# A Fourier convolution's last tile: its scratch in three parts instead of four, and a different reload

## The chip, the cores and the metric

One core of one Trainium2 chip runs the whole program. The metric is the device time of one execution in microseconds; lower is better. The compute engines are TensorE (PE in the profile; its weight loads are listed apart as PEld), VectorE (DVE), ScalarE (ACT) and GpSimd (POOL). SyncE (SP) issues most DMA transfers, ScalarE's queue (ACTq) a few. Engines run in parallel and wait for each other through semaphores.

## The reference

The reference convolves an image with a 7 x 7 kernel through Fourier transforms, circularly, over 96 input and 96 output channels:

```python
H = W = 224; C = 96; K = 7
x: (1, H, W, C) bf16        w: (K, K, C, C) bf16

wp = jnp.pad(w, ((0, H - K), (0, W - K), (0, 0), (0, 0)))
Xf = rfft2(x as float32, axes=(1, 2))
Wf = rfft2(wp as float32, axes=(0, 1))
Yf = jnp.einsum('bhwi,hwio->bhwo', Xf, Wf)
y  = irfft2(Yf, s=(H, W), axes=(1, 2)).astype(bfloat16)
```

## The kernel before, in words

The kernel does not transform the whole image. It cuts the 224 rows into NJ = 8 blocks of B = 28 rows and transforms each block, with 6 rows of overlap, along the rows only, to NS = 17 pairs of values (an index s from 0 to 16, each with two parts r). Along the columns it convolves directly, with a fast scheme of short taps. The 224 columns are cut into NT = 7 tiles of 32 columns; a tile has TW = 16 column pairs (index w), each with an even and an odd column.

For each tile t three stages follow:

- Stage A (`a_jobs`, `f_jobs`) multiplies the rows of the image by the transform matrix Fm into the tile xf.
- Stage B (`b_round`, one call for each s) multiplies sums of xf (the J tiles, made by VectorE) by the transformed weights WF, in about forty products of 96 columns a round, and puts the result into yf: 128 partitions are (w, j), and a row of yf is s. Every three s (`YGRP`, `YGRPL`) a *put* writes yf to a scratch tensor in DRAM, laid out as w, j, s, (r, column parity, channel).
- Stage C reads the scratch back with j, s and r on the partitions (the *reload*; each row of one w is 384 bytes) and multiplies by the inverse matrix G, which gives pixels. They are evicted as bf16 and stored to `out`.

Stage C of a tile normally runs as small jobs among the rounds of the next tiles. Round by round the order is written out by hand: lists of jobs with due times (`add`, `pace`), and every engine's instructions keep program order (`_Ordered`).

The last tile, t = TL = 6, has no later rounds to hide in. Its scratch is a set of tensors, cut along s by `SLAST` (line 37), here (0, 9, 12, 15, 17). Part 0 (`scra`, s 0 to 8) is reloaded early, in round s = SA + 2 = 11 (lines 964 to 967), into two views `tl_a[0]` and `tl_a[1]` (line 720) of a free xf buffer, one for each half of the row blocks (g = 0: j 0 to 3, g = 1: j 4 to 7). Each half has KA = 72 rows (4 blocks x 9 s x 2), widened to KAP = 80 with eight rows of the other half, for which the matrix GA has zeros. Parts 1 to 3 (`scrb`) are reloaded after the rounds by `load_b` (lines 723 and 724), one DMA each, into `tl_b`, 128 rows in all: 48, 48 and 32. The puts of the last tile's first five groups (three s each) are issued from ScalarE's queue (`puts`, lines 659 and 696), the last one, of s 15 and 16, from SP.

After the rounds the program issues, in this order: the remaining jobs of stage C for tile 5 (lines 971 and 972), `load_b` for each part (974 and 975), four stores of tile 5's pixels held back till now (`outs`, 976), and the last tile's own stage C. That needs sixteen results (g, q) of 112 x 384. Each is the sum of two products: `first` (GA with part 0, contraction over part 0's rows) and `second` (GB with the 128 rows of the other parts). Eight `first` products run ahead, into the eight banks of PSUM. Then WARM = 26 *fillers*, products of zeros that add nothing to the last bank, keep PE at work until the reloads land. Then the `second` products follow, each with its eviction, interleaved with the eight `first` products that are left; every two results make one store, eight in all.

GA and GB are made from G by small copies through DMA (`g_parts`, lines 726 to 737), one for each round of tiles 3 and 4 (lines 962 and 963) until none is left.

Of the kernel before, what the change touches and what calls it, by code (L numbers as in the profile page):

```python
# [8 lines left out]
BF16 = mybir.dt.bfloat16  # L9
# [5 lines left out]
B = 28  # L15
# [18 lines left out]
PGRP = ((0, 5), (5, 8), (8, 11), (11, 14), (14, 17))  # L34
YGRP = ((0, 3), (3, 6), (6, 9), (9, 12), (12, 15), (15, 17))
YGRPL = ((0, 3), (3, 6), (6, 9), (9, 12), (12, 15), (15, 17))
SLAST = (0, 9, 12, 15, 17)
SA = SLAST[1]
YMAX = 3
YBUF = 4  # L40
# [5 lines left out]
SH3 = (0, 8, 17)  # L46
MERGE = ()
NP2 = 0
WARM = 26
HEAD = ("w",) * 6 + ("x0", "w", "w", "h0", "h1", "w", "w", "x1", "w", "w")  # L50
W1 = 30
ZC = 48
# [12 lines left out]
def kernel(  # L65
# [7 lines left out]
    _, H, W, C = x.shape  # L73
    assert tuple(w.shape) == (KT, KT, C, C) and C == 96 and H == NJ * B and W % (2 * TW) == 0
    NT = W // (2 * TW)
    TL = NT - 1
# [29 lines left out]
    VE, SE, GE, TE, DE = (_Ordered(e) for e in (nc.vector, nc.scalar, nc.gpsimd, nc.tensor, nc.sync))  # L106
# [9 lines left out]
    def bank():  # L116
        return pools["psb"].tile([128, 512], F32, name="pb")
# [30 lines left out]
    def dma(out_ap, in_ap):  # L148
        return DE.dma_start(out=out_ap, in_=in_ap)
# [7 lines left out]
    G = cpool.tile([3 * FR, 3 * B], BF16, name="Gm")  # L157
    KA = 4 * 2 * SA
    NL = len(SLAST) - 1
    KB = [NJ * 2 * (SLAST[i + 1] - SLAST[i]) for i in range(1, NL)]  # L160
    RB = [sum(KB[:i]) for i in range(NL - 1)]
# [33 lines left out]
    def load_x(t, jg):  # L195
        return load_rows(xbuf(t, jg), jg, t * 2 * TW, 2 * TW)
# [208 lines left out]
    def diff(s):  # L405
        def f():
            load["v"] += 60 + C * NTAP / 1.92
            w0, w1, w2 = (WF[0:C, slot(s, r)].rearrange("i t o -> i (t o)") for r in range(3))
            VE.tensor_tensor(out=w2, in0=w0, in1=w1, op=ALU.subtract)
        return f  # L410
# [113 lines left out]
    def then_load(f, t, jg):  # L524
        def g():
            f()
            if t < NT:
                load_x(t, jg)
        return g
# [65 lines left out]
    def b_round(t, s, mid, end, ydve=False, planes=()):  # L595
# [90 lines left out]
        if s == y1 - 1:  # L686
            dst, yo0 = scr_tiles[t], 0
            if t == TL:
                i = sum(s >= v for v in SLAST[1:])
                dst, yo0 = scr_tiles[(t, i)], SLAST[i]  # L690

# [8 lines left out]
    scr_tiles = {}  # L700
# [15 lines left out]

    TW2 = 2 * TW * C
    tl_all = xf_bufs[(TL + 1) % 2].rearrange("c p r s w j -> c (p r s w j)")
    KAP = -(-KA // 16) * 16
    tl_a = [tl_all[0:KAP, g * TW2:(g + 1) * TW2].rearrange("p (w e) -> p w e", e=2 * C) for g in range(2)]  # L720
    tl_b = tl_all[:, 2 * TW2:3 * TW2].rearrange("p (w e) -> p w e", e=2 * C)

    def load_b(i):
        dma(tl_b[RB[i]:RB[i] + KB[i]], scr_tiles[(TL, 1 + i)].rearrange("w j s (r e) -> (j s r) w e", r=2))

    def g_parts():
        for g in range(2):
            for j in range(4):
                p = g * (KAP - KA) + j * 2 * SA
                dma(GA[p:p + 2 * SA, g, j * B:(j + 1) * B], G[0:2 * SA, 0:B])  # L730
                yield
        for j in range(NJ):
            for i in range(NL - 1):
                s, s1 = SLAST[i + 1:i + 3]
                n = 2 * (s1 - s)
                dma(GB[RB[i] + j * n:RB[i] + (j + 1) * n, j // 4, j % 4 * B:(j % 4 + 1) * B], G[2 * s:2 * s1, 0:B])
                yield
# [105 lines left out]
    def fills(qs, k):  # L843
        def f():
            for q in qs:
                pace(q, k)
        return f
# [3 lines left out]
    def add(a, b, jobs):  # L851
        qs.append([a, b, jobs, len(jobs)])
# [15 lines left out]
    for r in range(NS + LAG):  # L868
        if r == 0:
            for i in range(1, PGRP[0][1]):  # L870
                add(max(2 * i - 3, 0), 2 * i - 1, [diff(i)])
            for i in range(N5, REAL[1]):
                add(2 * i - (3 if i % 3 == 0 else 2), 2 * i - (i % 3 == 0), [diff(i)])
            add(0, 4, fj[1][0] + fj[1][1])
            add(8, 12, fj[2][0] + fj[2][1])
        if r == 2:
            new_xf(1, SH2[0], SH2[1])
        for p in range(3):
            if r == (1, 3, 6)[p]:
                if p:  # L880
                    new_xf(1, SH2[p], SH2[p + 1])
                else:
                    xf_tiles[1] = xf_bufs[1]
                fj = f_jobs(1, p)
                if p == 2:
                    for jg in range(2):
                        fj[jg][-1] = then_load(fj[jg][-1], 2, jg)
                add((4, 7, 12)[p], (7, 11, 15)[p], fj[0] + fj[1])
        for p in range(2):
            if r == SH3[p + 1] + 1 - p:  # L890
                new_xf(2, SH3[p], SH3[p + 1])
                fj = f_jobs(2, p)
                if p:
                    for jg in range(2):
                        fj[jg][-1] = then_load(fj[jg][-1], 3, jg)
                add(2 * r, 2 * r + (12, 5)[p], fj[0] + fj[1])
        if r == PGRP[-2][1] + 1:
            assert not any(q[2] for q in qs[:len(PGRP) - 1])
            wtmp_cm.__exit__(None, None, None)
            t_pool = ctx.enter_context(tc.tile_pool(name="tt", bufs=NTT, side="right"))  # L900
            t2_pool = ctx.enter_context(tc.tile_pool(name="tt2", bufs=1, side="right"))
            yo_pool = ctx.enter_context(tc.tile_pool(name="yo", bufs=2, side="right"))
            g_pool = ctx.enter_context(tc.tile_pool(name="gp", bufs=1, side="right"))
            GA = g_pool.tile([KAP, 2, 4 * B], BF16, name="GA")
            GB = g_pool.tile([128, 2, 4 * B], BF16, name="GB")
            GE.memset(GA[:], 0.0)
            GE.memset(GB[:], 0.0)
        if r == 3:
            g_fin()
        for t in range(2):  # L910
            s = r - LAG * t
            if not 0 <= s < NS:
                continue
            now = bursts.pop((r, t), ())
            now = jit(*now) if now else []
            now, rest = rest + now[:2], now[2:]
            both = LAG <= r < NS
            b_round(t, s, fills(qs, 2 * r + (t if both else 0)), fills(qs, 2 * r + (t if both else 1)), False, now)
            if r == 0:
                for d in load_x(1, 1):  # L920
                    tc.add_manual_dep(d.ins, held_x.ins.name, SYNC, reason="second half behind the first products")
# [8 lines left out]
    for t in range(2, NT):  # L930
        if t == TL:
            scr_tiles[t] = None
            scr_tiles[(t, 0)] = dr_pool.tile([TW, NJ, SA, 4 * C], BF16, name="scra")
            for i in range(1, NL):
                scr_tiles[(t, i)] = dr_pool.tile([TW, NJ, SLAST[i + 1] - SLAST[i], 4 * C], BF16, name=f"scrb{i}")
        else:
            scr_tiles[t] = dr_pool.tile([TW, NJ, NS, 4 * C], BF16, name="scr")
        qs = []
        if t + 1 < NT:
            add(4 if t == 2 else 0, 26, a_jobs(t + 1))  # L940
        nold, nnew = CQ[t]
        k1 = 2 * NS if t < TL else 2 * NS - 8
        k0 = {2: 15, TL: 6}.get(t, 3)
        km = k0 + -(-(k1 - k0) * nold // (nold + nnew))
        add(k0, km, cj[:nold])
        cn = c_jobs(t - 1)
        cj = cn[nnew:]
        add(km, k1, cn[:nnew])
        plan = {}
        for g, (s0, s1) in enumerate(JGB):  # L950
            if g + 1 < len(JGB) or t + 1 < NT:
                plan[s0 if g + 1 < len(JGB) else s0 - 1] = g
        for s in range(NS):
            now = ()
            if s in plan:
                g = plan[s]
                now = jit(t, g + 1) if g + 1 < len(JGB) else jit(t + 1, 0)
            if s == 2 and t == 2:
                queue_c(0)
            if s == (3 if t in (2, TL) else 2):  # L960
                queue_c(t - 1)
            if t in (3, 4):
                next(gp, None)
            if t == TL and s == SA + 2:
                sv = scr_tiles[(TL, 0)].rearrange("w j s (r e) -> (j s r) w e", r=2)
                for g in range(2):
                    dma(tl_a[g], sv[g * (2 * KA - KAP):g * (2 * KA - KAP) + KAP])
            b_round(t, s, fills(qs, 2 * s), fills(qs, 2 * s + 1), bool(now) or (t == TL and s >= NS - 3), now)
    tail[0] = 1
    load["v"], load["a"] = 1000.0, 0.0  # L970
# [12 lines left out]

    def first(g, q):
        pc = bank()[0:M4, 0:4 * C]
        TE.matmul(pc, lhsT=GA[:, g], rhs=tl_a[g][:, 2 * q:2 * q + 2, :].rearrange("p w e -> p (w e)"), start=True, stop=False)
        return pc

    def second(g, q, pc, yo):
# [3 lines left out]
    live = {k: first(*k) for k in order[:8]}  # L993
    for _ in range(WARM):
        TE.matmul(live[order[7]].rearrange("p (a b) -> p a b", a=3), lhsT=wu[:, 0:M4], rhs=wu[:].unsqueeze(1).to_broadcast([128, 3, 128]),
                  start=False, stop=False)
# [44 lines left out]
```

## Time and profile before

| | us |
|---|---|
| median of the runs | 263.75 (263.49 to 264.52) |
| profiled execution | 263.47 |
| its span, first to last instruction | 261.7 |
| PE busy | 252.0 (96%) |
| DVE busy | 218.4 (83%) |
| ACT busy | 196.7 (75%) |
| POOL busy | 97.6 (37%) |
| DMA, mean rate over the span | 179 GB/s |

Times in the profile are microseconds from the span's start. A row of the timeline has the start, the length, the engine, the operation with its tiles, and in brackets the idle time before it and what ended that. In a row of the chain the work is the one that the next step waited for. A DMA's issue is listed on the queue that issues it (SPq, ACTq); its data follow later, on sixteen DMA engines that all queues share, as packets. All lines of the kernel appear as L99, since a helper there records every operation, so that groups are told apart by their tiles: pb is a bank of PSUM, wu the zeros of the fillers, scra and scrb the parts of the last tile's scratch, tt the stores' buffers.

### The profile page before, as it was taken

The numbers are of one execution on the slowest core, as the hardware profiler recorded it, in microseconds if no ns is written. First come the engines' busy times: TensorE is split into PE (matmuls) and PEld (weight loads), VectorE is DVE, ScalarE is ACT, GpSimd is POOL, SyncE is SP. The second block draws the span as 40 slices with busy tenths as digits, with TensorE's granted clock in tenths as the row PEclk, the third lists the DMA queues.
The fourth block names the chain that finished last, engine by engine and source line by source line (L and its number), as shares of the span: only waits on it lengthen the run. The fifth ranks groups of instructions, "written<-read, shape, count | busy, mean of one in ns | idle before, by whom it ended". The sixth has DMA issues, their size and how long they took to land.

```text
span 261.7 us, 11987 instructions
## 1 busy us (share of the span) xinstructions
PE 252.0 (96%) x5054; PEld 233.2 (89%) x5054; DVE 218.4 (83%) x462; ACT 196.7 (75%) x470; POOL 97.6 (37%) x152
## 2 busy tenths in 40 slices
PE   8999999999999999999999999999999999989983
PEld 2889999999989999989999998999999999979652
DVE  6799998899999889868887788878989799989724
ACT  8889978697745967988988799887988853555423
POOL 7782224464656633232223322334123423423000
PEclk9999999999999999999999999999999999999999
DMA  7995104611111697997967596878849842886996
GB/s 177 272 186 135 48 6 140 177 48 48 48 51 71 183 255 138 302 286 192 271 188 222 143 278 206 212 200 255 275 139 193 288 140 83 206 232 185 236 249 201
DMA packets 47278, 46.88 MB, mean 179 GB/s; under 512 B 35696, under 2 KB 38452, under 8 KB 47224
## 3 DMA queue, kind: packets, MB, share of 16 engines
q1 hardware_dynamic: 46504, 44.64, 62.6%
q10 hardware_dynamic: 720, 1.47, 1.7%
q8 instruction: 39, 0.64, 1.1%
q14 instruction: 15, 0.12, 0.2%
HBM read 24.76 MB, written 21.33 MB: 176 GB/s over the span
## 4 chain that ended last, share of the span: by engine, by line
PE 74%; DVE 10%; DMA 8%; issue 4%; ACT 1%; POOL 1%; SPq 1%; DVEq 0%; ACTq 0%
PE pb L99 68%; PE ps L99 6%; DVE J L99 5%; DMA xn<-in_x_dram 3%; DVE WF L99 2%; DMA tt<-scr 2%; DMA xf<-scrb 2%; DMA scrb<-yf 1%; DVE v L99 1%; POOL yf L99 1%; DVE yf L99 1%; DMA scr<-yf 1%; DVE u L99 1%; SPq L99 1%; ACT xf L99 0%
## 5 line engine op out<-in xcount | busy, mean ns | idle before, releaser
L99 PE MATMUL pb<-WF,J 96*128 96x96 bf16 x2821 | 162.4, 206 | 2.1 <-DVE u L99 0.8
L99 PEld LDWEIGHTS <-J 96*128 96x128 bf16 x2821 | 138.0, 98 | 11.0 <-issue 3.7
L99 POOL TENSOR_TENSOR yf<-v,u 128x384 bf16<-128x384 f32 x79 | 81.4, 1044 | 139.7 <-issue 86.3
L99 ACT CAST xf<-pb 96x408 bf16<-96x408 f32 (+6 forms) x140 | 65.1, 492 | 3.4 <-PE pb L99 1.4
L99 PE MATMUL pb<-WF,xf 96*128 96x96 bf16 x952 | 59.9, 206 | 0.2
L99 DVE TENSOR_TENSOR J<-xf 96x456 bf16<-96x456 bf16 (+3 forms) x85 | 56.0, 698 | 0.0
L99 PEld LDWEIGHTS <-xf 96*128 96x128 bf16 x952 | 47.1, 98 | 1.0 <-PE ps L99 0.6
L99 PE MATMUL pb<-Fm,xn 118*128 118x136 bf16 (+4 forms) x576 | 43.8, 203 | 0.2 <-DMA xn<-in_x_dram 0.2
L99 PE MATMUL pb<-tt,Gm 102*84 102x384 bf16 (+1 forms) x132 | 32.0, 326 | 0.5 <-DVE yf L99 0.4
L99 ACT CAST yo<-pb 84x384 bf16<-84x384 f32 (+1 forms) x61 | 26.2, 482 | 6.2 <-PE pb L99 6.2
L99 PEld LDWEIGHTS <-xn 118*128 118x128 bf16 x576 | 28.6, 97 | 0.5 <-issue 0.4
L99 ACT CAST J<-pb 84x384 bf16<-84x384 f32 (+1 forms) x64 | 27.5, 491 | 0.0
L99 DVE TENSOR_TENSOR J<-J 96x912 bf16<-96x912 bf16 (+2 forms) x42 | 25.4, 604 | 0.0
L99 ACT CAST WF<-pb 96x480 bf16<-96x480 f32 x42 | 21.3, 566 | 0.1
L99 PEld LDWEIGHTS <-wq 128*128 128x128 bf16 (+1 forms) x288 | 19.7, 148 | 0.2
L99 DVE TENSOR_TENSOR yf<-v,u 128x384 bf16<-128x384 f32 x26 | 15.2, 583 | 0.9
L99 PE MATMUL pb<-wq 128*128 128x120 bf16 x192 | 15.3, 224 | 0.0
L99 DVE TENSOR_TENSOR WF<-WF 96x960 bf16<-96x960 bf16 x15 | 14.0, 931 | 1.4 <-ACT WF L99 1.3
L99 PEld LDWEIGHTS <-Gm 102*84 102x84 bf16 (+1 forms) x132 | 11.3, 117 | 1.6 <-issue 0.6
L99 PEld LDWEIGHTS <-wu 128*112 128x112 bf16 (+1 forms) x49 | 6.2, 128 | 6.4 <-issue 3.9
L99 ACT COPY xf<-xf 96x816 bf16<-96x816 bf16 (+4 forms) x18 | 10.8, 659 | 0.0
L99 DVE CAST tt<-pb 112x384 bf16<-112x384 f32 x8 | 4.2, 555 | 6.6 <-PE pb L99 6.2
(397 smaller groups left out, 256.9 us busy)
## 6 DMA issues: line engine op xcount, KB each, us to landing
scr<-yf SPq DMA_DIRECT2D x30, 288.0 KB
xn<-in_x_dram SPq DMA_DIRECT2D x12, 672.0 KB
tt<-scr SPq DMA_DIRECT2D x24, 336.0 KB
out_dram<-yo SPq DMA_DIRECT2D x12, 252.0 KB
out_dram<-J SPq DMA_DIRECT2D x12, 252.0 KB
tt<-scr SPq DMA_DIRECT2D x6, 288.0 KB
wq<-in_w_dram SPq DMA_DIRECT2D x5, 288.0 KB
WF<-in_x_dram SPq DMA_DIRECT2D x2, 672.0 KB
```

The costliest lines, as they stand in the source:

```text
L99: r = fn(*a, **k)
```

## The change

The last tile's scratch is cut into three parts instead of four, so that s 9 to 14 are one tensor and one reload of 96 rows; its puts stay three s each. Part 0's reload brings both halves g side by side, 72 rows with 32 elements of 384 bytes each, in two DMAs that are cut at row 64; GA loses its padding and its second copy. `first` reads its columns of half g with a step. GA and GB need 4 + 16 small copies instead of 8 + 24. The fillers are 18 instead of 26.

```diff
-SLAST = (0, 9, 12, 15, 17)
+SLAST = (0, 9, 15, 17)
...
-WARM = 26
+WARM = 18
...
-    KAP = -(-KA // 16) * 16
-    tl_a = [tl_all[0:KAP, g * TW2:(g + 1) * TW2].rearrange("p (w e) -> p w e", e=2 * C) for g in range(2)]
+    tl_a = tl_all[0:KA, 0:2 * TW2].rearrange("p (w g e) -> p w g e", g=2, e=2 * C)
...
     def g_parts():
-        for g in range(2):
-            for j in range(4):
-                p = g * (KAP - KA) + j * 2 * SA
-                dma(GA[p:p + 2 * SA, g, j * B:(j + 1) * B], G[0:2 * SA, 0:B])
-                yield
+        for j in range(4):
+            dma(GA[j * 2 * SA:(j + 1) * 2 * SA, j * B:(j + 1) * B], G[0:2 * SA, 0:B])
+            yield
...
-            GA = g_pool.tile([KAP, 2, 4 * B], BF16, name="GA")
+            GA = g_pool.tile([KA, 4 * B], BF16, name="GA")
...
             if t == TL and s == SA + 2:
-                sv = scr_tiles[(TL, 0)].rearrange("w j s (r e) -> (j s r) w e", r=2)
-                for g in range(2):
-                    dma(tl_a[g], sv[g * (2 * KA - KAP):g * (2 * KA - KAP) + KAP])
+                sv = scr_tiles[(TL, 0)].rearrange("w (g j) s (r e) -> (j s r) (w g) e", g=2, r=2)
+                ta = tl_a.rearrange("p w g e -> p (w g) e")
+                for p0, p1 in ((0, KA // 16 * 16), (KA // 16 * 16, KA)):
+                    dma(ta[p0:p1], sv[p0:p1])
...
     def first(g, q):
         pc = bank()[0:M4, 0:4 * C]
-        TE.matmul(pc, lhsT=GA[:, g], rhs=tl_a[g][:, 2 * q:2 * q + 2, :].rearrange("p w e -> p (w e)"), start=True, stop=False)
+        TE.matmul(pc.rearrange("p (w e) -> p w e", w=2), lhsT=GA[:], rhs=tl_a[:, 2 * q:2 * q + 2, g], start=True, stop=False)
         return pc
```

## The prediction

> **What bounds the kernel now.** I read the page's shares first (PE is busy for 96% of the span), then PE's own waits, then the chain that ended last, in order of time, and last the queues and the DMA packets of the final 25 us.
>
> PE's waits from 150 us to the end are three:
>
> ```profile
> PE pb L99 <- DMA xf<-scrb: 1.2, 1, 1.2
> PE pb L99 <- DVE u L99: 0.8, 1, 0.8
> PE pb L99 <- DVE yf L99: 0.4, 1, 0.4
> ```
>
> Columns: total us, times, longest. So up to the tail PE is the bound, and what the change takes off SP's queue before the tail (small DMAs into GA and GB) frees nothing that PE waits for. PE's instructions are the same in both programs, in the same order, but for eight fillers. The whole change is therefore read from the tail. Its chain (start, us, what):
>
> ```profile
> 244.94 3.54 DMA scrb<-yf
> 248.47 0.02 issue
> 248.49 4.40 DMA xf<-scrb
> 252.89 0.14 issue
> 253.03 3.96 PE pb L99 x22
> 256.99 0.02 issue
> 257.01 0.56 DVE tt L99
> ```
>
> The last put of the scratch, its reload, and then the closing products with their evictions and stores. No compute stands between 244.94 and 253.03: whatever makes the last reload land later moves the end by as much. SP's queue issues the reloads, ACT's the two puts before the last:
>
> ```profile
> 239.32 0.33 ACTq L99 DMA_DIRECT2D scrb<-yf  x1
> 243.20 0.33 ACTq L99 DMA_DIRECT2D scrb<-yf  x1
> 238.54 1.01 SPq L99 DMA_DIRECT2D xf<-scra  x2
> 244.94 0.34 SPq L99 DMA_DIRECT2D scrb<-yf  x1
> 245.32 1.16 SPq L99 DMA_DIRECT2D xf<-scrb  x1
> 247.77 0.30 SPq L99 DMA_DIRECT2D xf<-scrb  x1
> 248.49 0.30 SPq L99 DMA_DIRECT2D xf<-scrb  x1
> SPq L99 <- DMA scrb<-yf: 1.2, 1, 1.2
> ```
>
> Three reloads of part b: that of s 9 to 11 goes at 245.32, before the last put has landed and with no wait for one; that of s 12 to 14 waits 1.2 us (the last row) for the put issued at 243.20, which thus lands at about 247.7; that of s 15 and 16 goes when the last put lands, 248.47. Now the packets, in five windows: 238.54 to 239.5, 239.2 to 242, 240.5 to 241.5, 246.9 to 248.75, 248.75 to 252.1:
>
> ```profile
> DMA packets 0, 0.00 MB, mean 0 GB/s; under 512 B 0, under 2 KB 0, under 8 KB 0
> DMA packets 1252, 0.48 MB, mean 170 GB/s; under 512 B 1252, under 2 KB 1252, under 8 KB 1252
> DMA packets 678, 0.26 MB, mean 260 GB/s; under 512 B 678, under 2 KB 678, under 8 KB 678
> DMA packets 718, 0.29 MB, mean 155 GB/s; under 512 B 707, under 2 KB 715, under 8 KB 718
> DMA packets 1421, 0.61 MB, mean 182 GB/s; under 512 B 1391, under 2 KB 1391, under 8 KB 1421
> ```
>
> A reload's packets are 384 B (one row of one w), so "under 512 B" counts them. First: after the first issue of the scra reload, no packet for 1.0 us. Second and third: its rate, 1252 in the 2.5 us from 239.5, at best 678 per us. Fourth: 707 of the first b reload's 768 packets pass before 248.75, in time in which the last put was still landing. Fifth: the other 1280 and the rest run at 1391 / 3.35 = 415 per us, until 252.1; the last reload lands 0.8 us after that.
>
> **The change, part by part.**
>
> *Parts 1 and 2 of the scratch become one (SLAST).* The puts stay as they are. The reload of s 9 to 14 is now one DMA of 96 rows x 16 = 1536 packets and waits for both ACT puts, the later of which lands at 247.7. So what went at 245.32 goes at 247.77; nothing before 247.77 fills the stretch of the fourth window. On SP, the last reload and four stores of earlier results are queued behind this waiting issue. The last reload's own wait ends at 248.47 anyway, 0.4 us after the 0.3 us issue; the stores wait behind the reloads in both kernels. PE's closing products wait for both reloads.
>
> Landing of the last reload: issue 247.77, plus 1.0 to the first packet (first window), plus 1536 + 512 = 2048 packets, plus 0.8 from last packet to landing. The rate lies between 415 per us (fifth window) and 678 (third). I take 450, the mean of the second and fifth windows, 2643 packets in 5.85 us, since both are long stretches of reloads alone and 678 never held for long: 4.55 us. Sum 254.12 against 252.89: **+1.23 us**. Ends: 678 gives 3.0 us, so 252.6 (-0.3); 415 gives 4.93, so 254.5 (+1.6).
>
> *The reload of part a in one transfer of 32 elements a row, cut at row 64.* Two times 80 x 16 = 2560 packets become 64 x 32 + 8 x 32 = 2304: 256 fewer, at 450 per us 0.57 us of all engines. What this can buy is an earlier landing of the second ACT put, which ran through the same engines from 243.2 to 247.7 (4.5 us, against 3.54 for the last put in the chain). Bounds 0 to 0.57; I take **-0.3**, the middle, as no row shows which engine was last. The Trainium skill, page "DMA: Bandwidth & Descriptors", section "Why a DMA increments its semaphore by 16 and not by 1", says that a transfer from this queue runs on the largest number of engines, up to 16, that divides its outer dimension, on the lowest-numbered ones. By it the eight rows sit on eight engines, which carry 128 + 32 = 160 packets, as many as 2 x 80 before, and the credit would be 0 and the sum +1.23; no view here shows engines singly.
>
> The first eight GA products now need both transfers where four needed one. Before, they ran from 245.77 and their banks came free only until the last evictions at 247.23. If the eight rows land as late as the last packets of part a allow (29 packets after 245.5, plus 0.8: 246.4), the products end by 246.4 + 8 x 0.169 = 247.75 instead of 247.6. That costs nothing, as PE afterwards stands still anyhow; without that cover it would be 0.2 us. A product has 384 columns as before; 72 rows instead of 80 change no duration.
>
> *18 fillers instead of 26.* 26 took 4.39 us, 0.169 each; PE then waited 1.2 us:
>
> ```profile
> 247.45 4.39 PE L99 MATMUL pb<-wu 128*112 128x384 bf16 x26
> 253.03 0.99 PE L99 MATMUL pb<-xf,GB 128*112 128x384 bf16 x5 [1.19 <-DMA xf<-scrb]
> ```
>
> They end about 250.5 instead of 251.84. No gain, since PE waits for the reload; the idle gap grows from 1.2 to 253.9 - 250.5 = 3.4 us. That is free unless PE's clock falls in it (a rival).
>
> *Fewer GA and GB copies* (8 + 24 become 4 + 16), smaller GA memset: nothing, PE waits for none of it, and POOL is busy for 37%. Were that cover gone, 12 issues of some 0.35 us would count 4 us on SP, spread over 34 rounds of tiles 3 and 4.
>
> **Sum.** +1.23 - 0.3 = +0.9 us. From the closing products on all moves together, so the profiled execution's 263.47 (span 261.7, 1.8 around it) becomes 264.4. That execution lies 0.28 under the median of the runs, 263.75; forecast on the median 263.75 + 0.9 = **264.65**.
>
> **Rivals.**
>
> *Slow reloads, no credit.* All 2048 packets at 415 per us and the put as late as before: +1.6, 265.4. For it: the fifth window is the nearest stretch, the same tensor at the same hour. Against it: scra's first reload was faster.
>
> *The clock falls in the gap.* At the start the trace shows the price: 13 matmuls of 512 columns took 5.35 us in the window 1.00 to 6.40, 0.42 each, so 0.31 for 384 columns, where a closing product starts every 0.165 us. 24 closing products cost 24 x 0.15 = 3.5 us more, of which the evictions' lag hides about 0.5: +3.0 on top of +0.9, 267.65. It decides once the gap is long enough; before it was 1.2 us and the products behind it kept full rate, and no gap of this program is near 3.4. The Trainium skill, "TensorE: Matmul & The Clock Gate", section "What's actually happening", gives a free-running window of about 3.4 us, idle through one of which halves the clock. By that, a gap of 3.4 us is at the edge and a longer one catches a whole window only at times.
>
> *Faster: the second ACT put lands early.* Mechanism: with fewer packets ahead of it, the put issued at 243.20 takes 3.54 us as the last one did, landing at 246.74, 1.0 us earlier. With 450 per us the reloads then land at 253.1, +0.2; at the 678 rate at 251.6, -1.3, so 262.4. It ends below before when the put lands by 246.5 at 450 per us, or with the put as late as before, when the reloads run above 620 per us. For it: the third window. Against it: 256 packets pay 0.57 us at most.
>
> *The merged reload costs nothing* because the first b reload was held up anyway (its issue took 1.16 us where others take 0.30): then the stream merely continues and the change is -0.3 to +0.3, 263.75. Against it: 707 packets had passed by 248.75.
>
> **How the numbers follow.** Forecast case (+0.3 to +1.3) 0.43; slow reloads (+1.3 to +1.9) 0.22; clock 0.12; nothing (-0.3 to +0.3) 0.14; faster 0.09, of which 0.06 below -1.3. 0.5% of 263.75 is 1.3 us, about what a measurement of this kernel can tell from no change. Slower by more: 0.22 + 0.12 and a little of the forecast case, 0.36; faster by more: 0.06; within: 0.58. The range leaves out the clock case and the deeper half of the faster one: from -0.85 (262.9) to slow reloads with the put half a us later than before and some of a fallen clock, +2.45 (266.2).
>
> **What would show it.** After: one 96-row reload issued at about 247.5, the last at 248.2 to 248.5; few packets from 246.5 to 248.5; the last reload's step in the chain about 5.3 us long instead of 4.40; PE's wait on it about 3.4 us instead of 1.2; the closing products starting at about 253.9 and 0.165 us apart. Wrong would be: a second ACT put landing before 246.7, a packet rate above 600 per us through the reloads, or products 0.31 us apart.

## The result and the profile after

The changed kernel takes 265.46 us (median of 14 runs, 264.13 to 267.40), the kernel before 264.29 in the runs taken with it. The ratio is 1.0056, 95% interval 1.0034 to 1.0079: slower by 1.5 us, between 0.9 and 2.1. All ratios compare fast executions alone: those more than 1.5% above the fastest of their kernel are left out, here 267.72 and 268.32 of the kernel before. The forecast was +0.9 us, slower, with 0.5% as what can be told from no change; the result lies just beyond that mark. The profiled execution took 264.96 (span 263.2, before 261.7).

The chain that ended last, kernel after (start, us, what):

```profile
244.96 4.13 DMA scrb<-yf
249.09 0.02 issue
249.11 5.24 DMA xf<-scrb
254.35 0.14 issue
254.48 3.96 PE pb L99 x22
```

The shape is that of before, and so is the closing stretch: 3.96 us for the same 22 products. The last put takes 4.13 us instead of 3.54, and the last reload 5.24 instead of 4.40. Together they are 1.43 us longer, and the span is 1.5 us longer. This compares one execution of each kernel; how much these steps vary comes below. SP's queue in the timeline, and its wait from 244 to 250 (total, times, longest), kernel after:

```profile
238.54 2.82 SPq L99 DMA_DIRECT2D xf<-scra  x2
244.96 0.35 SPq L99 DMA_DIRECT2D scrb<-yf  x1
248.64 1.12 SPq L99 DMA_DIRECT2D xf<-scrb  x2
```

```profile
SPq L99 <- DMA scrb<-yf: 3.2, 1, 3.2
```

The first b reload is gone from 245.3. Both reloads stand behind one wait of 3.2 us for the second ACT put, which landed at 248.6, 0.9 us later than before. The packets in the windows 246.9 to 248.75 and 249.45 to 253.5:

```profile
DMA packets 93, 0.12 MB, mean 63 GB/s; under 512 B 29, under 2 KB 77, under 8 KB 93
DMA packets 2101, 0.86 MB, mean 212 GB/s; under 512 B 2077, under 2 KB 2077, under 8 KB 2101
```

Where 707 packets of the first reload had passed, 29 small ones pass now. Then all 2048 (and a few others of that size, 2077 in all) run in 4.05 us, 513 per us. PE's waits and its last groups before the closing products:

```profile
PE pb L99 <- DMA xf<-scra: 2.1, 1, 2.1
PE pb L99 <- DMA xf<-scrb: 0.3, 1, 0.3
```

```profile
248.07 1.59 PE L99 MATMUL pb<-xf,GA 72*112 72x384 bf16 x8 [2.11 <-DMA xf<-scra]
249.45 4.70 PE L99 MATMUL pb<-wu 128*112 128x384 bf16 x18
254.48 0.99 PE L99 MATMUL pb<-xf,GB 128*112 128x384 bf16 x5 [0.33 <-DMA xf<-scrb]
```

Two things here were not forecast. PE waits 2.1 us for part a, and the 18 fillers take 4.70 us, longer than 26 did (4.39). The granted clock explains the fillers. Columns: stretch, us, then busy time and count of PE, PEld, DVE, ACT and POOL, then the granted clock, the DMA share and GB/s:

```profile
246.00:248.00 2.00, 0.00 (x0) 0.00 (x0) 1.26 (x3) 0.62 (x2) 0.00 (x0) 1.00 0.47 148
248.10:249.30 1.20, 1.20 (x8) 0.97 (x9) 0.00 (x0) 0.00 (x0) 0.00 (x0) 1.00 0.03 10
249.31:252.70 3.39, 3.39 (x13) 2.27 (x12) 0.00 (x0) 0.00 (x0) 0.00 (x0) 0.50 0.94 199
252.80:254.30 1.50, 1.36 (x9) 0.80 (x7) 0.00 (x0) 0.00 (x0) 0.00 (x0) 1.00 1.06 271
254.40:258.50 4.10, 4.02 (x24) 3.03 (x24) 3.22 (x7) 2.87 (x7) 0.00 (x0) 1.00 0.88 308
```

After the idle 2 us the clock stays full for 1.2 us, is 0.50 for 3.4 us, and is full again when the closing products start. In this execution the fillers had taken the whole penalty: they ended 0.33 us before the closing products could begin.

So three candidates are left for the loss: the merged reload, part a's reload (late by itself, and in the way of the puts), and the clock together with the 18 fillers. The experiments part them. For the clock I use each execution's mean granted clock: one stretch of 3.4 us at half makes 0.5 x 3.4 / 263 = 0.0065, so 0.994 or less counts below as *fallen*. This is a rough mark, as a half clock after the last product lowers the mean too (to 0.996 in the profile with 34 fillers below). In the kernel after that is 12 of 14 executions; in the kernel before 5 of the 83 that ran beside the experiments, and those 5 had a median of 266.1 against 263.4.

### The profile page after: what moved, and what is told of

It reads as the page before. It is cut to its first block, busy times and chain, and to the rows that moved or that the text cites. A ratio compares the mean times of both kernels' runs of the same rounds, so it can differ in the third digit from the quotient of the medians.

```text
span 263.2 us, 11957 instructions
## 1 busy us (share of the span) xinstructions
PE 252.2 (96%) x5046; PEld 233.1 (89%) x5046; DVE 218.3 (83%) x462; ACT 196.5 (75%) x470; POOL 97.6 (37%) x152
## 4 chain that ended last, share of the span: by engine, by line
PE 80%; DVE 11%; DMA 4%; issue 2%; ACT 1%; DVEq 0%; ACTq 0%
PE pb L99 74%; PE ps L99 6%; DVE J L99 5%; DVE WF L99 2%; DMA xf<-scrb 2%; DMA scrb<-yf 2%; DVE v L99 1%; DVE yf L99 1%; DVE u L99 1%; DVE xf L99 1%; ACT xf L99 0%; DVE tt L99 0%; ACT WF L99 0%; DVEq L1034 0%; ACT tt__5999 L99 0%
## 5 line engine op out<-in xcount | busy, mean ns | idle before, releaser
L99 PEld LDWEIGHTS <-wu 128*128 128x128 bf16 (+1 forms) x41 | 6.1, 152 | 6.8 <-issue 3.8
## 6 DMA issues: line engine op xcount, KB each, us to landing
out_dram<-yo SPq DMA_DIRECT2D x12, 252.0 KB
out_dram<-J SPq DMA_DIRECT2D x12, 252.0 KB
```

The source lines that it names most:

```text
L99: r = fn(*a, **k)
```

## Experiments

**The merged reload alone.**

```diff
-SLAST = (0, 9, 12, 15, 17)
+SLAST = (0, 9, 15, 17)
```

(on the kernel before)

> The kernel before with the merged b reload alone (part a's reload and 26 fillers as before). Theory of two terms (the merged reload goes late, and the eight-row transfer makes the puts land late): the second ACT put lands as before, at 247.7, and the merged reload goes at once; with the 2048 packets in the 4.0 us that they took in the changed kernel the last reload lands at 247.7 + 0.9 + 4.0 + 0.85 = 253.5 instead of 252.9: +0.6 us on the kernel before (ratio 1.002). If the merge were the whole loss: +1.5 us (1.0056). Rival, that the late GA products and the half clock are the loss: 0, since GA's products start at 245.8 here and the clock stays full.

Measured: ratio 1.0073 (1.0047 to 1.0098), +1.9 us, clock fallen in 3 of 12. The merge alone costs as much as the whole change, and not by the clock: the nine executions with a full clock have a median of 264.8, those of the kernel before beside them 263.0. The end of its chain in the profile:

```profile
245.27 2.81 DMA scrb<-yf
248.08 0.02 issue
248.10 5.27 DMA xf<-scrb
```

The reload step is 5.27 us, like 5.24 in the changed kernel, with the put no later than before. The profile shows only +0.87 in this step, near the +0.6 expected; its execution, 263.96, is one of the fastest of the twelve. The median of all twelve, 265.2, is 1.2 us above it, and no trace shows where.

**Part a's reload and 18 fillers, without the merge.**

```diff
-SLAST = (0, 9, 15, 17)
+SLAST = (0, 9, 12, 15, 17)
```

(on the changed kernel)

> The changed kernel with the b reloads in three as before (part a's new reload and 18 fillers stay). Theory of two terms: the second ACT put lands at 248.6 and the last put at 249.1 as in the changed kernel, the first b reload goes before them, the last reload lands some 4.5 us after the last put, at 253.6: +0.7 us on the kernel before. If the merge were the whole loss: 0. The eight GA products start at about 248 behind a wait of some 2 us in any case, and fillers run at 0.32 us apart for a while.

Measured: 1.0038 (1.0008 to 1.0068), +1.0 us. The size is about that expected, the reason is not. The chain of its profile no longer holds a put or a b reload at all:

```profile
238.27 8.13 DMA xf<-scra
246.41 0.14 issue
246.54 11.54 PE pb L99 x48
```

From part a's landing on PE never waits again: eight GA products, 18 fillers and 22 closing products take 11.54 us, as the clock is at half from 246.5 to 253.4. The last reload had landed at 252.0 and had to wait for the fillers. PE had stood still for only 1.17 us before the clock fell; in the 3.41 us before the fall it was busy for 1.79 (the granted clock is the third number from the end):

```profile
243.13:246.54 3.41, 1.79 (x11) 0.96 (x9) 3.38 (x8) 2.90 (x8) 0.00 (x0) 1.00 0.92 262
246.55:253.36 6.81, 6.81 (x22) 4.65 (x23) 0.12 (x1) 0.00 (x0) 0.00 (x0) 0.50 1.06 252
```

The clock fell in 10 of 12 executions.

**18 fillers alone.**

```diff
-WARM = 26
+WARM = 18
```

(on the kernel before)

> The kernel before with 18 fillers alone. Both theories: PE waits 2.5 us for the last reload instead of 1.2, the end does not move: 0 us. If a gap of 2.5 us before the closing products drops the clock: closing products 0.31 us apart and up to +3 us, in executions where the clock's window falls so.

Measured: 1.0032 (1.0005 to 1.0059), +0.8 us. The clock fell in 7 of 12 executions; those have a median of 264.8, the other five 263.0, so the price is 1.8 us where it is paid, and nothing otherwise. The profile fell on an execution with a full clock (263.01); PE waits 1.65 us there for the last reload:

```profile
252.42 0.99 PE L99 MATMUL pb<-xf,GB 128*112 128x384 bf16 x5 [1.65 <-DMA xf<-scrb]
```

**26 fillers in the changed kernel.**

```diff
-WARM = 18
+WARM = 26
```

(on the changed kernel)

> The changed kernel with 26 fillers instead of 18. If the clock halves for 3.4 us after the wait for part a, as in the profile of the changed kernel: fillers from 249.5 run 0.32 us apart till 252.7, the other 16 at 0.169 end at about 255.4, after the last reload (254.35): closing products about 1.1 us later than in the changed kernel, +2.6 us on the kernel before (1.010). If the clock stays full: fillers end at 253.9, no cost, +1.5 us as the changed kernel.

Measured: 1.0075 (1.0042 to 1.0107) against 1.0056 for the changed kernel, intervals that overlap; the step expected, to 1.010, did not come in the median. In the profile, where the clock was at half for 6.8 us, it did: the chain is PE alone from part a's landing on.

```profile
238.54 8.48 DMA xf<-scra
247.01 0.14 issue
247.15 12.85 PE pb L99 x56
```

**The eight rows first.**

```diff
-                for p0, p1 in ((0, KA // 16 * 16), (KA // 16 * 16, KA)):
+                for p0, p1 in ((KA // 16 * 16, KA), (0, KA // 16 * 16)):
```

(on the changed kernel)

> The changed kernel with the two transfers of part a's reload in the other order, the eight rows first. If the eight rows land late because they queue behind 64 rows and the first of the last ACT puts on half of the engines: both land by about 246.3, PE's wait for part a falls from 2.1 to about 0.4 us and the clock stays full more often; the second ACT put still lands at 248.0 to 248.6, as the half of the engines that has the eight rows carries as much as before. Time: 0 to -0.8 us on the changed kernel. If the transfer of eight rows is slow by itself: GA's products still start at about 248, no change.

Measured: 1.0078 (1.0051 to 1.0105), four runs. GA's products start at 246.04 without a wait, so the eight rows are slow only in second place. The second ACT put lands at 247.7, as in the kernel before, earlier than the 248.0 to 248.6 expected. The gain did not follow. The fillers now end at 250.6 and PE waits 3.07 us for the merged reload. The clock fell in all four executions, in the profile into the closing products instead of the fillers:

```profile
250.70:253.70 3.00, 0.00 (x0) 0.03 (x1) 0.00 (x0) 0.00 (x0) 0.00 (x0) 1.00 1.17 251
253.70:259.40 5.70, 5.69 (x24) 3.94 (x24) 3.31 (x7) 2.89 (x7) 0.00 (x0) 0.70 0.75 251
```

The 24 closing products take 5.7 us instead of 4.1 at a mean clock of 0.70. That is the rival of the prediction as it was described, in another kernel than the one it was meant for.

**Late, or merged?**

```diff
-    for i in range(NL - 1):
+    for i in (1, 0, 2):
         load_b(i)
```

(on the kernel before)

> The kernel before with its three b reloads issued in the order 2, 1, 3, so that the reload of s 9 to 11 goes late, behind the second ACT put, but nothing is merged and nothing else changes. If the merge costs time because the first reload goes late (theory): as the merged kernel with 26 fillers, +1.5 to +2.0 us on the kernel before, ratio 1.006 to 1.007. If the single transfer of 96 rows is what is slower (rival): 0 to +0.3 us.

Measured: 1.0100 (1.0071 to 1.0130), +2.6 us, clock fallen in 3 of 6. Three separate reloads, none merged, with the first behind the second put: as slow as the merge or slower. The last reload's step in its chain:

```profile
248.88 5.21 DMA xf<-scrb
```

The last put had landed at 248.3; the last reload's issue, the third in a row, adds 0.6 us to this step. So the late start of the first reload is enough for the loss, without a transfer of 96 rows. PE waited 2.47 us here and the clock stayed full, though PE was busy for only 1.71 in these 3.41 us:

```profile
250.05:253.46 3.41, 1.71 (x11) 1.09 (x9) 0.00 (x0) 0.00 (x0) 0.00 (x0) 1.00 1.31 190
```

**PE kept at work through both gaps, with the merge.**

```diff
-WARM = 18
+WARM = 30
...
         pc = bank()[0:M4, 0:4 * C]
+        for _ in range(14 if (g, q) == (0, 0) else 0):
+            TE.matmul(pc.rearrange("p (a b) -> p a b", a=3), lhsT=wu[:, 0:M4], rhs=wu[:].unsqueeze(1).to_broadcast([128, 3, 128]),
+                      start=True, stop=True)
```

(on the changed kernel)

> The changed kernel with 14 more fillers ahead of the first GA product and 30 instead of 18 behind the GA products, so that PE has work over both gaps. If the clock falls because PE stands still in the wait for part a: the granted clock stays at full in nearly all executions. If the fallen clock is a good part of the loss: 0.5 to 1 us faster than the changed kernel, ratio to the kernel before 1.002 to 1.004. If the merged reload alone sets the end (rival): as the changed kernel, ratio 1.005 to 1.007, in spite of the full clock.

Measured: 1.0065 (1.0039 to 1.0090); the clock fell in none of six executions. Its PE row in the windows, 8.5 us of it:

```profile
245.50:254.00 8.50, 8.50 (x54) 6.77 (x53) 1.51 (x4) 0.88 (x3) 0.00 (x0) 1.00 0.82 192
```

A full clock throughout, and the loss is still there. (Of the profiled execution's loss some 0.2 us may be the fillers': the last reload lands at 253.66 and the closing products start at 254.01, where 0.14 us lie between the two elsewhere.) So the loss does not need a fallen clock. In the changed kernel the clock may still add to it: six of the 14 executions, at a mean clock of 0.982 or 0.983, have a median of 265.8, the other eight 264.7. No trace shows one of the six, so this is not shown.

**PE kept at work, without the merge.** The changed kernel with the last edit's 14 fillers and these two lines.

```diff
-SLAST = (0, 9, 15, 17)
+SLAST = (0, 9, 12, 15, 17)
...
-WARM = 18
+WARM = 22
```

> The changed kernel with the b reloads in three as before, 14 fillers ahead of the first GA product and 22 behind the GA products: part a's new reload alone, with PE at work through its wait. If the loss of part a's reload with 18 fillers (ratio 1.0038) is the fallen clock: full clock in nearly all executions and 0 to +0.4 us on the kernel before, ratio 1.000 to 1.0015. If the puts that land late cost of themselves: still +0.7 to +1.0 us, 1.003 to 1.004, at full clock.

Measured: 1.0002 (0.9969 to 1.0036), the clock fallen in none of 12. With PE kept at work, part a's new reload costs nothing that can be told (by the interval at most 0.9 us), though in this profile too GA's products start late, at 249.0, where all of the tail stands 0.95 us later than in the kernel before, and though the fillers hold the closing products up by 0.8 us (the last reload had landed at 252.9):

```profile
246.74 2.44 PE L99 MATMUL pb<-wu 128*112 128x384 bf16 x14
249.01 1.47 PE L99 MATMUL pb<-xf,GA 72*112 72x384 bf16 x8
250.32 3.74 PE L99 MATMUL pb<-wu 128*112 128x384 bf16 x22
253.89 0.98 PE L99 MATMUL pb<-xf,GB 128*112 128x384 bf16 x5
```

Two kernels that differ in the merge and some fillers, at a full clock: 1.0065 with it, 1.0002 without, in intervals that do not overlap.

**34 fillers in the kernel before.**

```diff
-WARM = 26
+WARM = 34
```

> The kernel before with 34 fillers, which end at about 253.2, when the last reload lands. If the wait of 1.2 us for the reload is what lets the clock fall in some executions of the kernel before (and a wait of 2.5 us in more, with 18 fillers): the granted clock is at full in every execution and the median is 0 to 0.4 us below the kernel before, ratio 0.998 to 1.000. If fillers only delay the closing products: +0.3 us, 1.001.

Measured: 1.0020 (0.9996 to 1.0044), clock fallen in 2 of 12. No gain: the kernel before loses its clock in only 5 of 83 executions, and 34 fillers delay the closing products a little. In its profile the last reload lands at 252.67 and the closing products begin at 253.17.

**Three tries at a faster kernel.** Each reloads part a in two portions, s 0 to 5 early and s 6 to 8 after the last of their puts, and keeps three b reloads. The edits are on the changed kernel and are shown in part: the scratch tensors, part b's offsets and the copies into GA and GB follow SLAST. The first keeps 18 fillers.

```diff
+SLAST = (0, 6, 9, 12, 15, 17)
...
+            if t == TL and s in (10, SA + 2):
+                i = int(s == SA + 2)
+                sv = scr_tiles[(TL, i)].rearrange("w (g j) s (r e) -> (j s r) (w g) e", g=2, r=2)
+                ta = tl_a.rearrange("p w g e -> p (w g) e")
+                dma(ta[8 * SLAST[i]:8 * SLAST[i + 1]], sv)
```

> A version of its own: three b parts as before; part a in two parts, s 0 to 5 (48 rows, both halves) reloaded in round 10, ahead of the last puts, and s 6 to 8 (24 rows) in round 11; 18 fillers. By the reading that the puts land late because they share the engines with part a's reload: 768 instead of 2304 packets are left after 238.5, the second ACT put lands at about 246.2 and the last put at about 247, the last reload at about 251, 1.5 us earlier than before: ratio 0.994 to 0.996. If the puts' landing is set by something else: 0, ratio 1.000 or, with 18 fillers and a falling clock, 1.003.

Measured: 1.0080 (1.0046 to 1.0114), clock fallen in all seven executions. The early reload was not early. It stands on SP behind two groups of stores and then waits 0.9 us, till 238.18, for the put of s 6 to 8, which it does not read. The second reload is a transfer of 24 rows. SP's timeline, what it waited for, and PE's timeline:

```profile
235.25 1.58 SPq L100 DMA_DIRECT2D out_dram<-J  x1
236.94 0.35 SPq L100 DMA_DIRECT2D out_dram<-yo  x1
238.19 1.39 SPq L100 DMA_DIRECT2D xf<-scra  x2
```

```profile
SPq L100 <- DMA scra<-yf: 0.9, 1, 0.9
```

```profile
249.12 2.78 PE L100 MATMUL pb<-xf,GA 72*112 72x384 bf16 x8 [3.30 <-issue]
```

By the semaphores' updates the 24 rows landed in twelve increments of their own (sixteen for 48 rows), the last at 249.03, 10.4 us after the issue; GA's products waited 3.3 us. The next two cut the second portion into two transfers of 16 rows that overlap by 8 (sixteen increments each in the trace) and issue the first in round 9 or 8, with 24 fillers:

```diff
-                dma(ta[8 * SLAST[i]:8 * SLAST[i + 1]], sv)
+                for d0, s0, n in (((0, 0, 48),), ((48, 0, 16), (64, 8, 16)))[i]:
+                    dma(ta[d0:d0 + n], sv[s0:s0 + n])
```

> A version of its own, mending the last one: part a in two reloads, both spread over all sixteen engines (48 rows; then two of 16 rows that overlap by 8, for which GA has zeros), the first issued in round 9, among the stores of tile 5 at about 234 to 235.5; b reloads in three, 24 fillers. If the puts land late because of what part a leaves on the engines after 238.5: 1024 packets there instead of 2560, second ACT put at about 246.3, last reload at about 251.5: ratio 0.994 to 0.997. If the puts' landing does not follow: 1.000 to 1.003.

> The same with the first reload of part a issued in round 8, ahead of three stores of tile 5. If the earlier place frees the engines further: as the last or 0.5 us faster. If it delays a reload that tile 5's products wait for: PE waits before 245 and the time is 0 to 2 us above the kernel before.

Measured in round 9: 1.0075 (1.0048 to 1.0101). In round 8: five of six executions above 268 us, so that no ratio is given; the sixth took 263.48. The profile of round 8 is of one of the five, so that it tells only what happened there. SP's queue in the profile of each, round 9 first:

```profile
236.25 0.73 SPq L100 DMA_DIRECT2D xf<-scra  x1
237.08 1.72 SPq L100 DMA_DIRECT2D out_dram<-yo  x1
239.62 0.97 SPq L100 DMA_DIRECT2D xf<-scra  x2
```

```profile
233.53 0.66 SPq L100 DMA_DIRECT2D xf<-scra  x1
234.28 8.79 SPq L100 DMA_DIRECT2D out_dram<-J  x3
243.16 0.34 SPq L100 DMA_DIRECT2D out_dram<-yo  x1
243.55 0.97 SPq L100 DMA_DIRECT2D xf<-scra  x2
```

What SP waited for, in round 9 from 240 to 247 and in round 8 from 234 to 243.6:

```profile
SPq L100 <- DMA scrb<-yf: 5.8, 1, 5.8
SPq L100 <- DMA scra<-yf: 4.4, 1, 4.4
```

In round 9 SP waits till 246.4 for the first ACT put, so that the last put goes out at 246.46. In the kernel before it goes at 244.94, as soon as its data are ready, which would have been about 245.4 here. In round 8, 4.4 of the 8.79 us are a wait of the third store for a put of part a, issued at 234.41 and landed at 242.73; the second portion goes at 243.55 instead of 238.5, and GA's products wait 3.3 us for it. Neither transfer uses what it waits for, and neither did the early reload of round 10; in the traces each of the three has the same semaphore as the put that it waits for. The premise, that the puts would follow the number of packets left after 238.5, was hardly tested. In round 9 the packets did not move ahead (from 238.5 to 243.2, 1712 under 512 B pass, 1704 in the kernel before). In round 8 they did (769), and the second ACT put took 3.9 us from issue to landing, no less than the shortest, 3.9, in a kernel with part a's reload as before. None of the versions beats the kernel before.

## Why the prediction was right, and where its steps were wrong

The direction and the main mechanism were right: the merged reload goes behind the second ACT put, and nothing fills the engines in its place. The profile shows what was named: no packets where the first reload's had been, one issue for 96 rows, a reload step of 5.24 us where "about 5.3" was forecast. The order experiment shows that lateness alone is enough for the loss, and the pair at a full clock (1.0065 and 1.0002) that without the merge no loss is left that can be told. The profiles agree: from the issue of the last put to the landing of the last reload, the five in which the first b reload goes early (the kernel before, part a's reload with 18 fillers and with PE kept at work, 18 and 34 fillers) take 7.0 to 8.0 us, the six in which it goes late 8.1 to 9.4.

The number owes something to luck. With the credit the second ACT put was forecast at 247.4 and the packets at 4.55 us; the put came 1.2 us later and the packets were 0.5 us faster, so that two errors cancelled in part. The single losses do not add up either: 1.9 for the merge and 1.0 for part a's reload with 18 fillers, 1.5 for both. The profile suggests why, as there the fillers' delay falls into time in which PE waits for the merged reload anyway.

*The term of the merge was sized too small.* It was +1.23, with ends -0.3 and +1.6. Alone it measured +1.9 (1.2 to 2.6). In the profile of the merge alone the reload's step is +0.87. About half of what the medians lose to the merge is thus seen in traces; where the rest arises stays open.

*The credit of -0.3 for fewer packets was not borne out.* In the profile of the changed kernel the second ACT put landed at 248.6 instead of 247.7. From issue to landing it took 3.9 to 4.7 us in five profiles with part a's reload as before and 4.0 to 5.4 in five with the new one, 64 rows first: 0.4 us more on average, with overlap, so that not even the sign is sure. The sentence from the Trainium skill, "DMA: Bandwidth & Descriptors", "Why a DMA increments its semaphore by 16 and not by 1", had put the credit at 0, and the traces bear out what it states of the number of engines: by the semaphores' updates the eight rows landed in eight increments, 24 rows in twelve, 64 rows in sixteen. What was missed may be that the eight engines lag behind the rest, in the puts as well: with the eight rows in second place the increments of the second ACT put come in two groups (ten up to 246.8 and six from 247.4 in the changed kernel, eight and eight with 26 fillers in it); with the eight rows first, fifteen come from 245.7 to 246.6 and the last at 247.7. No view shows which engine made which increment, so this is not shown. At the median it costs nothing that can be told (1.0002).

*"The eight rows land by 246.4" was wrong.* They landed at 247.9. I had taken the last packets of the kernel before for those of the kernel after, though the eight rows now stood in second place; first in order they land at 241.7. The step was priced at nothing because PE would stand still afterwards. That cover held for the wait itself, but the wait lowered the clock, which the step left out.

*"18 fillers: no gain" was not contradicted for the changed kernel (26 there gave 1.0075), and its condition was the rival.* The rival said that the clock falls in the gap before the closing products; in the changed kernel's profile it was another gap, ahead of the GA products, and the fillers took the penalty, so that PE's wait for the last reload was 0.3 us and not the 3.4 forecast. The rival's price for a product at the fallen clock, 0.31 us, was right (0.32 in the profile with the eight rows first). Its total was 3.0 and is 1.8 where the fillers alone are changed. The point from which it decides was set at a gap near 3.4 us; in fact 2.1 us were enough, and with part a's reload alone 1.17. Of the Trainium skill, "TensorE: Matmul & The Clock Gate", "What's actually happening", the trace bears out the length (the clock was at half for 3.4 us, or for 6.8) but not that the PE must be idle for a whole window: in the 3.41 us before the clock fell, PE was busy for 1.3 in the changed kernel, and for 1.79 in the profile of part a's reload.

*Slow reloads, no credit* named +1.6, close to what was measured, but by a rate that did not occur: 415 packets per us, where 513 were measured.

*The faster rival* asked for the second ACT put by 246.5 or packets above 620 per us. Neither came: 248.6 and 513. *The rival that the merge costs nothing* fell with the first experiment.

## What to carry to other kernels

When the last transfers are a chain of write, wait and read back, do not merge an early read with a late one: here the part that could go early was worth more than the issue that was saved, and its place in time was enough to explain a loss of this size. Filler work at the end has to be judged by the granted clock of many executions, not by one profile, and every wait ahead of the fillers counts as a gap as well. A saving is to be measured with the other term neutralised: part a's reload looked like 1 us of loss until PE was kept busy, and then no loss could be told. When a queue stands still, look at what each of its transfers waits for before calling the issue slow.

## What the runs showed of the hardware that was not expected

- All changes of the granted clock in a profile lie a whole number of 3.41 us apart. In six profiles the clock fell before the last product, and in the 3.41 us before the fall PE had been busy for 0.4 to 1.8 us. In the order experiment a stretch with 1.71 left it full. So the length of a gap alone does not decide: 1.17 us were once enough and 2.47 once not. The clock then stayed at half for 3.4 us, or for 6.8.
- Which gap costs what depends on the execution. The kernel before with 18 fillers, whose gap is 1.7 us in its profile, lost its clock in 7 of 12.
- A transfer that landed in eight or twelve increments landed late when it stood behind others: 8.8 us for eight rows in second place against 3.5 in first, and 10.4 us for 24 rows.
- SP's queue stood still behind transfers whose data it did not need: 4.4 us of the 8.79 that three stores took, and about 1.0 us by which a last put went out later than its data were ready, each time for a put with the same semaphore in the trace.
